# Spreading the last w_out steps of a fused attention and FFN kernel, and holding its second products to a later tick

## The chip, the core and the metric

One core of a Trainium2 chip runs the whole kernel. The metric is the device time of one execution in microseconds (us), as the median of several runs. The engines are named as in the profile: PE (matrix products), DVE and POOL (elementwise work, reductions), ACT (elementwise functions, and a DMA queue of its own), SP (only issues DMAs).

## What is computed

Eight batches of eight attention heads (576 rows, 64 columns each) with a bias that comes from a running sum of `s`, and on the result a gated FFN from 512 to 1536 and back:

```python
def _attn_ref(q, k, v, s):
    scores = scale * np.matmul(q, k.transpose(0, 1, 3, 2))
    cum = np.cumsum(np.maximum(s, 0.0), axis=-1)
    bias = -(cum[:, :, :, None] - cum[:, :, None, :])
    scores = np.where(causal, -1000000000.0, scores + np.minimum(bias, 0.0))
    ...                                   # softmax
    return np.matmul(attn, v).astype(np.float32)

def _moe_ref(x, w_gate, w_val, w_out):
    gate = 1.0 / (1.0 + np.exp(-(x @ w_gate)))
    val = x @ w_val
    return (gate * val @ w_out).astype(np.float32)
```

`x` is the attention's output, 4608 tokens of 512. The three weights of the FFN arrive as float64.

## The kernel before

**Ticks.** 64 heads of five query tiles each make 320 ticks; the loop `for n in range(nticks + 12)` goes through them and emits, for each tick, the scores of one tile (`s_part`, L446 and L447), the bias and the maximum (L461, L471), exponentials (L474), the probabilities p in two halves (L478, L483, L491), their transposition by DMA (pt, L494), the product with v (`av_part`, L506 to L511) and, for a pair of heads, the x of the FFN: `x_part`, `split_x` (L517 to L529), whose last step is a DMA transposition into one of ten x slots. Heads of batch 0 run in another form (names with n_). Slots 0 to 4 exist from the start (NXE is 5); the others are made by `late_slots()` (L189), which closes the pool lp and opens another one in its room. lp holds ws0 (raw words of one weight step) and wa0 (decoded words). x8 and x9, for example, are first used as scratch for the squares of v of batch 2 (load L161 on SP, at ticks from VSQ on).

**FFN.** Tokens are cut into groups of 256; a unit is a group and one of 12 blocks of hidden columns. `ffn_in` multiplies x with w_gate and w_val (tile gv in PSUM, 24 matmuls for a whole group, L657), takes the tanh on ACT (th, L662) and the product on DVE (L664). The units of groups 0 and 1 leave this product in a big tile, t2f. `ffn_mid` scales it by hsc and splits it into two halves h (L672 on ACT, L673 on DVE), `ffn_out` multiplies with w_out (tile o, L687) and, after the 12th block, writes the group's rows by way of an output tile osb (L694, L695).

**Weight steps.** The float64 weights are decoded on the chip in 18 steps: 12 for w_gate and w_val, 6 (12 to 17) for w_out. Each step loads 1 MB of raw words (two DMAs, L253 and L260 on ACT's queue), decodes them (L272 on ACT, L273 to L275 on DVE; the last of them is the last reader of the raw words), sums their squares (L287 on ACT, L289 on POOL), makes a power of two (L125, L127) and writes two rounded halves (L292 on ACT, L293 on DVE; L293 is the last reader of the decoded words). `outroom` says for each of the six w_out steps where its raw words go, where its decoded words go, and behind which step its load may be issued. `hidden_scale()` needs the scales of all 18 steps and gives hsc (L309). No second product can start before it.

**Order.** A planner of the language puts the instructions of each engine in order: it takes the order in which the code emits them as an input, and its own estimate of time as another. Numbers such as ticks therefore do not set the order by hand. Before the change, steps 14 to 17 are emitted with the units of group 1, three steps ahead, which ends by tick 51; in the tick in which the 24th unit is emitted, `hidden_scale`, all 24 held second products and `late_slots` follow. Around that:

```python
outroom = [(4, 0, 0), (5, 0, 0), (0, 0, NF - 3), (3, 0, NF - 1), (5, 0, NF + 1), (0, 0, NF + 2)]
...
                while f >= NF and wnext["step"] < min(f + NF + WLA, len(wsteps)):
                    weight_step()
                emit_unit()
            if state["u"] == 2 * NF:
                hidden_scale()
                while state["o"] < 2 * NF:
                    emit_out()
                late_slots()
```

Of the kernel before, what the change touches and what calls it, by code (L numbers as in the profile page):

```python
# [8 lines left out]
F32 = mybir.dt.float32  # L9
F32R = mybir.dt.float32r  # L10
I32 = mybir.dt.int32
# [5 lines left out]
P = 128  # L17
# [6 lines left out]
def tile_attention_then_gated_ffn(  # L24
# [13 lines left out]
    NT, DM = out.shape  # L38
# [4 lines left out]
    NF = DFF // P  # L43
# [13 lines left out]
    cp = ctx.enter_context(tc.tile_pool(name="cp", bufs=1))  # L57
# [109 lines left out]
    def v_square_sum(b, c):  # L167
        t = vsq.pop((b, c))
        pin(nc.scalar.activation(t, t, AF.Square, accum_out=vss[b][:, c : c + 1]))
# [13 lines left out]
    fp = ctx.enter_context(tc.tile_pool(name="fp", bufs=2))  # L183
    lstack = ctx.enter_context(ExitStack())
    lp = lstack.enter_context(tc.tile_pool(name="lp", bufs=1))
    NX, NXE = 10, 5
    xslots = [cp.tile([P, 2, NTL * P], F16, name=f"x{i}") for i in range(NXE)] + [None] * (NX - NXE)

    def late_slots():  # L189
        lstack.close()  # L190
        xp = lstack.enter_context(tc.tile_pool(name="xp", bufs=1))
        for i in range(NXE, NX):
            xslots[i] = xp.tile([P, 2, NTL * P], F16, name=f"x{i}")
# [17 lines left out]
            c += n  # L211

    raw0 = lp.tile([P, 8 * P, 2], I32, name="ws0")
    dec0 = lp.tile([P, 8 * P], I32, name="wa0")
    flat = w2all.rearrange("p f l h x n -> p (f l h x n)").bitcast(I32)
    raw = [raw0] + [flat[:, i * 16 * P : (i + 1) * 16 * P].rearrange("p (n t) -> p n t", t=2) for i in range(2)]
    dec = [dec0] + [flat[:, i * 8 * P : (i + 1) * 8 * P] for i in range(4, 6)]
# [1 line left out]
    wsteps = [(0, f) for f in range(NF)] + [(1, f) for f in range(0, NF, 2)]  # L219
# [2 lines left out]

    for i in (1, 2):
        raw.append(t2big[:, 8 * i * GT : 8 * (i + 1) * GT].bitcast(I32).rearrange("p (n t) -> p n t", t=2))
    outroom = [(4, 0, 0), (5, 0, 0), (0, 0, NF - 3), (3, 0, NF - 1), (5, 0, NF + 1), (0, 0, NF + 2)]

    def room(n):

        o, f = wsteps[n]
        if o == 0:  # L230
            return raw[f % 3], dec[f % 3], n - 3
        i, j, last = outroom[f // 2]
        return raw[i], dec[j], last
# [61 lines left out]
    def inverse_weights(o, fs):  # L295
        inverse_pow2(invw[:, o, fs], wscale[:, o, fs])

    def hidden_scale():


        inverse_weights(1, slice(0, NF))
        g = wp.tile([P, NF], F32, tag="hsg", name="hsg")
        nc.vector.tensor_tensor(g, invw[:, 0], invw[:, 1], ALU.mult)
        m = wp.tile([P, 1], F32, tag="hsm", name="hsm")
        nc.vector.tensor_reduce(m, g, mybir.AxisListType.X, ALU.max)
        nc.vector.tensor_scalar(gmax, m, 2.0 ** -100, None, ALU.max)
        r = wp.tile([P, 1], F32, tag="hsr", name="hsr")
        nc.vector.reciprocal(r, gmax)
        nc.vector.tensor_scalar(hsc, g, r, 2.0 ** -16, ALU.mult, ALU.mult)  # L309
        out_scale(0)  # L310
# [3 lines left out]
    def out_scale(b):  # L314
        osc[b] = wp.tile([P, 1], F32, tag="osc", name=f"osc{b}", bufs=3)
        nc.vector.tensor_scalar(osc[b], gmax, sv[b][1], 2.0 ** 15, ALU.mult, ALU.mult)

    wnext = {"load": 0, "step": 0}

    def weight_step():  # L320
        n = wnext["step"]
        while n and wnext["load"] < len(wsteps) and room(wnext["load"])[2] < n:
            if not NF <= wnext["load"] < NF + 2:
                load_weight(wnext["load"])
            wnext["load"] += 1
        split_weight(n, decode_weight(n))
        wnext["step"] = n + 1
# [310 lines left out]
    def pieces_of(g):  # L638
        a, e = g * GT, min((g + 1) * GT, NT)
        r = []  # L640
        while a < e:
            b = a // S
            z = min(e, (b + 1) * S)
            r.append((a - g * GT, z - g * GT, b))
            a = z
        return r, e - g * GT
# [29 lines left out]
    def ffn_out(g, f):  # L676
        pcs, n = pieces_of(g)
        if g < 2:
            ffn_mid(g, f)
        h = hst.pop((g, f))  # L680
        for tt in range((n + P - 1) // P):
            m = min(P, n - tt * P)
            if f == 0:
                ops_[g, tt] = pp.tile([P, 512], F32, tag="o", name=f"o{g}_{tt}")
            ps = ops_[g, tt]
            for c, (hl, wl) in enumerate(((0, 0), (0, 1), (1, 0))):
                nc.tensor.matmul(ps[:m], h[:, hl, tt * P : tt * P + m], w2[f][:, wl],  # L687
                                 start=(f == 0 and c == 0), stop=(f == NF - 1 and c == 2))
            if f == NF - 1:
                o = fp.tile([P, DM], F32, tag="io", name=f"osb{g}_{tt}", bufs=2)  # L690
                for a, e, b in pcs:
                    a, e = max(a - tt * P, 0), min(e - tt * P, P)
                    if a < e:
                        nc.scalar.activation(o[a:e], ps[a:e], AF.Copy, scale=osc[b][a:e])  # L694
                nc.gpsimd.dma_start(out[g * GT + tt * P : g * GT + tt * P + m, :], o[:m])  # L695
                del ops_[g, tt]
# [3 lines left out]
    state = {"u": 0, "o": 0}  # L700
# [8 lines left out]
    def emit_out():  # L709
        if state["o"] < len(units):  # L710
            ffn_out(*units[state["o"]])
            state["o"] += 1
# [10 lines left out]
    NE, NOFF = 44, 87  # L723
    FPT = 1.5
    EARLY = 18
    VSQ = 65
    OUT = (22, 30)
    WLA = 3
    nticks = NTL * NH
    for n in range(nticks + 12):  # L730
# [13 lines left out]
        if 2 <= n < nticks + 2:  # L744
            a, z = divmod(n - 2, NTL)
# [5 lines left out]
        if 1 <= n < nticks + 1:  # L751
            a, z = divmod(n - 1, NTL)
# [7 lines left out]
        if 3 <= n < 3 + NTL * NN:  # L760
            with first():
                a, z = divmod(n - 3, NTL)
# [11 lines left out]
        if i < NH:  # L774
            p, j = divmod(i, 2)
# [80 lines left out]
            elif b == 1:  # L856
                if VSQ <= n < VSQ + vch:
                    v_square(2, n - VSQ)
                if VSQ + 5 <= n < VSQ + 5 + vch:
                    c = VSQ + 4 + vch - n  # L860
                    v_square_sum(2, c)
                if n == VSQ + 11:
                    v_scale(2)
# [12 lines left out]
        if n >= NE and state["u"] < 2 * NF:  # L876
            fdone = min(NF, int((n - NE + 1) * FPT))
            while state["u"] < 2 * fdone:
                f = state["u"]
                if f < NF and f % WLA == 0:  # L880
                    while wnext["step"] < f + WLA:
                        weight_step()
                    inverse_weights(0, slice(f, f + WLA))
                    ffn_scale(0, slice(f, f + WLA))
                while f == 8 and wnext["step"] < NF + 1:
                    weight_step()
                while f >= NF and wnext["step"] < min(f + NF + WLA, len(wsteps)):
                    weight_step()
                emit_unit()
            if state["u"] == 2 * NF:  # L890
                hidden_scale()
                while state["o"] < 2 * NF:
                    emit_out()
                late_slots()
        if (n - 30) % (NTL * H) == 0 and n >= 30 + NTL * H:
            ffn_scale((n - 30) // (NTL * H))
        m = n - (11 if n > 2 * NTL * H + 30 else 7)
# [40 lines left out]
```

## Time and profile before

| | us |
|---|---|
| median of 3 runs | 1154.59 |
| lowest and highest | 1151.61, 1155.06 |
| the profiled execution | 1150.75 |
| its span, first to last instruction | 1149.0 |
| PE busy | 1093.9 (95%) |
| DVE, ACT, POOL busy | 774.6, 748.6, 261.9 |

The span is 1.75 us shorter than the profiled execution's own time. All starts below are counted from the span's start. Idle time of an engine is the length of a stretch less its busy time in it; a wait names the instruction that stood still and what came last of what it waited for. A DMA's row on SP is the time that SP took to issue it, not the transfer.

### The profile page before, as it was taken

How to read it: one execution, taken by the hardware profiler on the slowest of the kernel's cores; microseconds unless marked ns; L12 is line 12 of the kernel's file. 1: busy time of each engine (PE TensorE's matmuls, PEld its weight loads, DVE VectorE, ACT ScalarE, POOL GpSimd, SP SyncE). 2: the span in 40 equal slices, each digit the busy share in tenths (PEclk: the TensorE clock that was granted, in tenths of full speed). 3: DMA queues.
4: the chain of work that ended last, by engine and by line, in shares of the span. 5: the costliest groups of instructions: out<-in, count | busy, mean ns of one | idle time of the engine just before them, and what ended most of it. 6: DMA issues, size and time to landing. Idle time of an engine off the chain costs nothing.

```text
span 1149.0 us, 30327 instructions
## 1 busy us (share of the span) xinstructions
PE 1093.9 (95%) x11644; PEld 856.3 (75%) x11644; DVE 774.6 (67%) x2393; ACT 748.6 (65%) x1465; POOL 261.9 (23%) x570
## 2 busy tenths in 40 slices
PE   6787889989999999999999999999999999999997
PEld 4566677758777887788777777778877887787775
DVE  6889899866777777775565677777777775222221
ACT  6989778667677777676665677767776765233222
POOL 5625233222132222121211122212222221000000
PEclk9879899999999999999999999999999999999999
DMA  9776778996989888778646488868887764000000
GB/s 266 214 212 164 178 144 183 185 186 135 165 170 174 165 173 169 141 146 145 137 81 136 89 183 164 162 145 181 145 162 144 142 123 88 13 20 19 1 19 19
DMA packets 445102, 157.62 MB, mean 137 GB/s; under 512 B 403551, under 2 KB 435295, under 8 KB 444958
## 3 DMA queue, kind: packets, MB, share of 16 engines
q1 hardware_dynamic: 418398, 127.12, 57.1%
q10 hardware_dynamic: 23040, 16.78, 4.9%
q0 software_dynamic: 3520, 11.80, 3.0%
q8 instruction: 91, 1.49, 0.6%
q14 instruction: 53, 0.43, 0.1%
HBM read 56.92 MB, written 9.58 MB: 58 GB/s over the span
## 4 chain that ended last, share of the span: by engine, by line
PE 51%; issue 25%; DMA 6%; DVE 5%; ACT 3%; POOL 2%; SPq 1%; POOLq 0%; ACTq 0%; DVEq 0%
PE gv L657 28%; PE o L687 14%; PE s L447 2%; PE s L446 2%; DMA v<-in_v_dram 2%; DMA qk<-in_q_dram 1%; POOL rl L461 1%; PE av L506 1%; PE av L508 1%; DVE e L471 1%; PE av L507 1%; DMA pt<-p 1%; SPq L420 1%; ACT e L474 1%; PE av L510 1%
## 5 line engine op out<-in xcount | busy, mean ns | idle before, releaser
L657 PE MATMUL gv<-x,w 128*128 128x256 f16 (+3 forms) x6912 | 613.5, 246 | 5.4 <-DVE t2f L664 2.9
L657 PEld LDWEIGHTS <-w 128*128 128x128 f16 x6912 | 534.0, 98 | 61.7 <-issue 5.3
L687 PE MATMUL o<-w2all,h 128*128 128x512 f16 x1296 | 314.8, 379 | 0.0
L461 POOL TENSOR_SCALAR_AFFINE_SELECT rl<-rl 128x64 f32<-128x64 f32 (+1 forms) x280 | 111.3, 398 | 519.6 <-DVE em L471 464.3
L474 ACT ACTIVATE e<-e,em 128x576 f32<-128x576 f32 x280 | 154.7, 554 | 92.5 <-DVE em L471 90.5
L687 PEld LDWEIGHTS <-h 128*128 128x128 f16 x1296 | 123.7, 98 | 108.0 <-issue 1.7
L662 ACT ACTIVATE th<-gv,scb 128x256 f32<-128x256 f32 (+3 forms) x288 | 111.2, 411 | 138.4 <-PE gv L657 137.6
L664 DVE SCALAR_TENSOR_TENSOR t<-th,gv 128x256 f32<-128x256 f32 x192 | 80.0, 417 | 132.8 <-ACT th L662 131.6
L471 DVE CUSTOM_DVE_ANT_0 e<-s,rl,qkcf 128x288 f32<-128x288 f32 x280 | 135.6, 485 | 29.9 <-PE s L447 24.5
L672 ACT ACTIVATE h<-t,hsc 128x256 f16<-128x256 f32 x192 | 96.6, 503 | 80.1 <-DVE t L664 80.0
L483 DVE SCALAR_TENSOR_TENSOR p<-e,p 128x384 f16<-128x384 f32 x224 | 101.9, 494 | 40.1 <-ACT p L478 39.3
L673 DVE SCALAR_TENSOR_TENSOR h<-t,hsc,h 128x256 f16<-128x256 f32 x192 | 93.1, 485 | 43.4 <-ACT h L672 43.0
L478 ACT ACTIVATE p<-e 128x1152 f16<-128x1152 f32 x112 | 112.1, 1001 | 3.2 <-DMA pt<-p 0.5
L506 PE MATMUL av<-v,pt 128*128 128x65 f16 x560 | 68.0, 193 | 5.3 <-DMA pt<-p 5.3
L446 PE MATMUL s<-T 128*128 128x288 f16 (+2 forms) x246 | 64.8, 281 | 5.2 <-DMA T<-qk 3.8
L695 POOL DMA_DIRECT2D out_dram<-osb x36 | 20.4, 566 | 212.1 <-ACT osb L694 211.2
L507 PE MATMUL av<-v,pt 128*128 128x64 f16 x560 | 68.0, 192 | 0.0
L508 PE MATMUL av<-v,pt 128*128 128x65 f16 x560 | 68.0, 194 | 0.0
L447 PE MATMUL s<-T 128*128 128x288 f16 (+2 forms) x246 | 61.8, 279 | 1.7 <-DMA T<-T 1.6
L506 PEld LDWEIGHTS <-pt 128*128 128x128 f16 x560 | 52.4, 97 | 11.8 <-DMA pt<-p 6.9
L409 POOL PARTITION_BROADCAST cr<-cr x63 | 58.1, 923 | 4.1 <-DMA cr<-cum_d 4.0
L455 DVE TENSOR_SCALAR rl<-cr,qkcf 128x576 f32<-128x576 f32 x56 | 29.1, 519 | 40.0 <-POOL cr L409 39.8
(155 smaller groups left out, 1440.7 us busy)
## 6 DMA issues: line engine op xcount, KB each, us to landing
out_dram<-osb POOLq DMA_DIRECT2D x36, 256.0 KB, 2.9
v<-v SPq DMA_DIRECT2D x56, 162.5 KB
v<-in_v_dram SPq DMA_DIRECT2D x64, 128.0 KB
T<-T SPq DMA_DIRECT2D x82, 72.0 KB
t2f<-in_v_dram SPq DMA_DIRECT2D x20, 288.0 KB
qk<-in_q_dram SPq DMA_DIRECT2D x17, 288.0 KB
qk<-in_k_dram SPq DMA_DIRECT2D x17, 288.0 KB
w2all<-in_moe_w_gate_dram ACTq DMA_DIRECT2D x7, 512.0 KB
```

What stands on the lines that cost most here:

```text
L446: nc.tensor.matmul(ps[:, : b_ - a], lhs, T[i][:, 0, a:b_], start=True, stop=False)
L461: nc.gpsimd.affine_select(rl[i][:, q0:w], rl[i][:, q0:w], pattern=[[-1, m]], compare_op=ALU.is_ge, fill=-MASKED if i < NN else MASKED, bas ...
L471: nc.vector.tensor_tensor_reduce(e_t[t][:, a:b_], ps[:, : b_ - a], rl[i][:, a:b_], c, init, ALU.add, ALU.min, acc)
L474: nc.scalar.activation(e_t[t][:, :w], e_t[t][:, :w], AF.Exp, bias=init, scale=-1.0)
L478: nc.scalar.activation(p_s[h_][:, 0], e_s[h_], AF.Copy, scale=PSCALE)
L483: nc.vector.scalar_tensor_tensor(flat[:, LOW[t] * P : (LOW[t] + t) * P], e_t[t][:, : t * P], PSCALE, flat[:, kb * P : (kb + t) * P], ALU.m ...
L506: nc.tensor.matmul(AV[i][:, t], hi, v_[:, D : 2 * D + 1], start=kb == 0, stop=False)
L657: nc.tensor.matmul(ps[:, gv, a:e], w1[f][:, cc, gv, wl], x_of(b, cc)[:, xl, c0 + a : c0 + e], start=(c == 0), stop=(c == 3 * NC - 1))
L662: nc.scalar.activation(th[:, a:e], ps[:, 0, a:e], AF.Tanh, scale=scb[b][:, f : f + 1])
L672: nc.scalar.activation(h[:, 0], t2, AF.Copy, scale=hsc[:, f : f + 1])
L673: nc.vector.scalar_tensor_tensor(h[:, 1], t2, hsc[:, f : f + 1], h[:, 0], ALU.mult, ALU.subtract)
L687: nc.tensor.matmul(ps[:m], h[:, hl, tt * P : tt * P + m], w2[f][:, wl], start=(f == 0 and c == 0), stop=(f == NF - 1 and c == 2))
```

## The change

1. x slots that exist from the start: six in place of five; four are left for `late_slots`.
2. A tile osb in the permanent pool takes the place of the output tiles and, as dec0, of wa0: the decoded words lie in the output's room. In lp only ws0 is left.
3. The last two of `outroom`: step 16 loads into ws0 behind step 14, step 17 into the same ws0 behind step 16. Before, they used part of t2f and ws0.
4. Steps 14 to 17 are emitted at ticks 50, 54, 58 and 62; `hidden_scale`, the held second products and `late_slots` at tick 66 (NOUT). The squares of v of batch 2 start at tick 68 and not 65.

```diff
-    NX, NXE = 10, 5
+    NX, NXE = 10, 6
@@
     raw0 = lp.tile([P, 8 * P, 2], I32, name="ws0")
-    dec0 = lp.tile([P, 8 * P], I32, name="wa0")
+    osb = cp.tile([P, 2, DM], F32, name="osb")
+    dec0 = osb.rearrange("p a n -> p (a n)").bitcast(I32)
@@
-    outroom = [(4, 0, 0), (5, 0, 0), (0, 0, NF - 3), (3, 0, NF - 1), (5, 0, NF + 1), (0, 0, NF + 2)]
+    outroom = [(4, 0, 0), (5, 0, 0), (0, 0, NF - 3), (3, 0, NF - 1), (0, 0, NF + 2), (0, 0, NF + 4)]
@@
-                o = fp.tile([P, DM], F32, tag="io", name=f"osb{g}_{tt}", bufs=2)
+                o = osb[:, tt % 2]
@@
-    VSQ = 65
+    NW, NOUT = 50, 66
+    VSQ = 68
@@
-                while f >= NF and wnext["step"] < min(f + NF + WLA, len(wsteps)):
+                while f >= NF and wnext["step"] < NF + 2:
                     weight_step()
                 emit_unit()
-            if state["u"] == 2 * NF:
-                hidden_scale()
-                while state["o"] < 2 * NF:
-                    emit_out()
-                late_slots()
+        while NF + 2 <= wnext["step"] < min(NF + 3 + (n - NW) // 4, len(wsteps)):
+            weight_step()
+        if n == NOUT:
+            hidden_scale()
+            while state["o"] < 2 * NF:
+                emit_out()
+            late_slots()
```

The lines of the changed kernel are one higher from L215 on (L310 is L309 of before). In the rows below, the digits behind a name are the planner's numbers of the tiles. On DVE, around the end of `hidden_scale` (gmax and hsr lead to hsc), there stood before, from row 412 on:

```order
L471 ISA em12_2_0_2934 128x1
L305 TENSOR_REDUCE hsm_2380<-hsg_2378 128x1
L306 TENSOR_SCALAR gmax_113<-hsm_2380 128x1
L293 SCALAR_TENSOR_TENSOR w2all_78<-wa0_137,wscale_111,w2all_78 128x1024
L308 RECIPROCAL hsr_2383<-gmax_113 128x1
L316 TENSOR_SCALAR osc0_2386<-gmax_113,vin0_328 128x1
L471 ISA e_0_79,em12_1_0_2949<-s12_1_0_2922,rl12_2814,qkcf6_2679 128x192
L471 ISA em12_1_0_2949 128x1
L316 TENSOR_SCALAR osc1_3132<-gmax_113,vin1_1006 128x1
L365 TENSOR_SCALAR qk0_7_2952<-qkt7_2941 128x2
L309 TENSOR_SCALAR hsc_112<-hsg_2378,hsr_2383 128x12
```

and now, from row 416 on:

```order
L665 SCALAR_TENSOR_TENSOR t2f_136<-th1_1_1934,gv1_1_1909 128x256
L131 TENSOR_SCALAR invw_110<-wscale_111 128x12
L472 ISA e_0_79,em12_0_0_2724<-s12_0_0_2692,rl12_2548,qkcf6_2385 128x64
L472 ISA em12_0_0_2724 128x1
L304 TENSOR_TENSOR hsg_2804<-invw_110 128x12
L306 TENSOR_REDUCE hsm_2806<-hsg_2804 128x1
L307 TENSOR_SCALAR gmax_113<-hsm_2806 128x1
L309 RECIPROCAL hsr_2809<-gmax_113 128x1
L317 TENSOR_SCALAR osc0_2812<-gmax_113,vin0_329 128x1
L317 TENSOR_SCALAR osc1_3126<-gmax_113,vin1_1007 128x1
L310 TENSOR_SCALAR hsc_112<-hsg_2804,hsr_2809 128x12
```

hsc moves from row 422 to row 426; the last L293 (step 17, reading the decoded words) moves from row 415 to row 434, behind hsc.

On ACT, step 17's raw words (the DMA into ws0) were issued before right behind the square of step 14 (wss14), from row 212 on:

```order
L287 ACTIVATE w2all_78,wss14_1886<-wa0_137 128x1024
L253 DMA ws0_136<-in_moe_w_out_dram 128x8x128
L474 ACTIVATE e_1_80<-e_1_80,em9_4_1_1557 128x576
L260 DMA ws0_136<-in_moe_w_out_dram 128x8x128
L662 ACTIVATE th0_0_1374<-gv0_0_1349,scb0_1347 128x256
```

Now the load that stands there is step 16's, and that of step 17 stands behind the square of step 16 (wss16), from row 252 on. Its reader, the first L273 of step 17, is row 267:

```order
L288 ACTIVATE w2all_78,wss16_2530<-osb_138 128x1024
L254 DMA ws0_137<-in_moe_w_out_dram 128x8x128
L261 DMA ws0_137<-in_moe_w_out_dram 128x8x128
L388 ACTIVATE qk16_12_2420<-qk32_6_2220,qksc6_2383 96x6x64
L390 ACTIVATE qk16_12_2420<-qk32_6_2220,qksc6_2383 96x6x64
L663 ACTIVATE th0_9_1794<-gv0_9_1769,scb0_1348 128x256
L475 ACTIVATE e_0_79<-e_0_79,em11_2_0_2523 128x320
L663 ACTIVATE th0_10_1822<-gv0_10_1797,scb0_1348 128x256
L293 ACTIVATE w2all_78<-osb_138,wscale_111 128x1024
L475 ACTIVATE e_0_79<-e_0_79,em11_1_0_2545 128x192
L475 ACTIVATE e_0_79<-e_0_79,em11_0_0_2559 128x64
```

The load moved from row 213 to row 253, 14 rows ahead of its reader; before, the reader was row 259.

On PE, the first second product o0_0 stood behind unit gv1_3, from row 1412 on:

```order
L657 LDWEIGHTS w1_3_69
L657 MATMUL gv1_3_2029<-x3_133,w1_3_69 128x256
L657 LDWEIGHTS w1_3_69
L657 MATMUL gv1_3_2029<-x3_133,w1_3_69 128x256
L687 LDWEIGHTS h0_0_2388
L687 MATMUL o0_0_2391<-w2all_78,h0_0_2388 128x512
L687 LDWEIGHTS h0_0_2388
L687 MATMUL o0_0_2391<-w2all_78,h0_0_2388 128x512
```

and now, from row 1460 on:

```order
L447 LDWEIGHTS T13_2575
L447 MATMUL s13_2_0_3050<-T13_2575 128x320
L448 LDWEIGHTS T13_2575
L448 MATMUL s13_2_0_3050<-T13_2575 128x320
L658 LDWEIGHTS w1_4_70
L658 MATMUL gv1_4_2002<-x3_133,w1_4_70 128x256
L658 LDWEIGHTS w1_4_70
L658 MATMUL gv1_4_2002<-x3_133,w1_4_70 128x256
L688 LDWEIGHTS h0_0_2814
L688 MATMUL o0_0_2817<-w2all_78,h0_0_2814 128x512
```

The first second product moved from row 1417 to row 1469, behind one more unit, gv1_4, and behind scores of head 13.

## Rows read from the trace of the kernel before

**Rows 1.** The page, section 1: engine, busy us, share of the span, instructions.

```profile
PE 1093.9 (95%) x11644; PEld 856.3 (75%) x11644; DVE 774.6 (67%) x2393; ACT 748.6 (65%) x1465; POOL 261.9 (23%) x570
```

**Rows 2.** Busy time by stage: stretch, its length, each engine, PEclk, DMA share, GB/s.

```profile
119.00:190.00 71.00, 59.89 (x621) 49.86 (x620) 64.77 (x197) 55.48 (x100) 22.64 (x43) 0.95 0.79 170
190.00:241.00 51.00, 47.72 (x477) 35.05 (x475) 42.73 (x148) 39.59 (x78) 15.93 (x31) 1.00 0.96 187
241.00:303.00 62.00, 57.65 (x724) 42.99 (x723) 42.51 (x135) 41.89 (x88) 14.31 (x30) 1.00 0.77 162
...
430.00:985.00 555.00, 555.00 (x6282) 436.88 (x6281) 388.98 (x1260) 371.22 (x723) 113.93 (x274) 1.00 0.72 139
...
145.00:165.00 20.00, 17.03 (x181) 14.56 (x179) 17.63 (x51) 15.39 (x28) 6.45 (x11) 1.00 0.68 136
165.00:190.00 25.00, 21.81 (x254) 18.58 (x252) 23.37 (x78) 19.79 (x37) 7.80 (x16) 1.00 0.77 165
```

**Rows 3.** Waits of PE, 119 to 190 us: us in total, times, longest us.

```profile
PE gv L657 <- DVE t2f L664: 2.9, 3, 1.7
...
PE nx_ps L629 <- DVE nx L615: 0.6, 1, 0.6
```

**Rows 4.** Waits of PE, 190 to 303 us.

```profile
PE s L447 <- DMA t2f<-t2f: 2.1, 1, 2.1
PE av L506 <- DMA pt<-p: 1.6, 1, 1.6
PE gv L657 <- DMA x<-x: 1.6, 1, 1.6
```

**Rows 5.** Instructions by tile (ws, w2all, hsc): ns min/median/max, first and last start.

```profile
L272 ACT ACTIVATE wa<-ws x6: 1111/1138/1157, 11.2 to 169.6; 128x1024 f32<-128x1024 f32 x6
L275 DVE SCALAR_TENSOR_TENSOR wa<-ws,wa x6: 1216/1219/1251, 14.7 to 176.9; 128x1024 int32<-128x1024 int32 x6
...
L260 ACTq DMA_DIRECT2D ws<-in_moe_w_out_dram x2: 682/768/854, 81.0 to 132.2; - x2
...
L293 DVE SCALAR_TENSOR_TENSOR w2all<-wa,wscale,w2all x6: 1258/1274/1285, 110.3 to 183.5; 128x1024 f16<-128x1024 f32 x6
...
L309 DVE TENSOR_SCALAR hsc<-hsg,hsr x1: 229/229/229, 185.4 to 185.4; 128x12 f32<-128x12 f32 x1
...
L687 PE MATMUL o<-w2all,h x1296: 377/379/380, 190.4 to 1142.0; 128*128 128x512 f16 x186
```

**Rows 6.** PE, from 231 us: start us, us, instruction, count.

```profile
231.21 1.58 PE L657 MATMUL gv<-x,w 128*128 128x256 f16 x13
```

**Rows 7.** ACT by line and shape, 160 to 190 us: count, busy us, mean ns.

```profile
L662 ACT ACTIVATE th<-gv,scb 128x256 f32<-128x256 f32 x8 | 3.7, 458 | 0.6 <-PE gv L657 0.6
...
L292 ACT ACTIVATE w2all<-wa,wscale 128x1024 f16<-128x1024 f32 x2 | 2.3, 1136 | 0.0
...
L387 ACT ACTIVATE qk<-qk,qksc 96x384 f16<-96x384 f32 x3 | 1.8, 614 | 1.4 <-DMA T<-qk 0.7 <-DVE qksc L371 0.7
...
L478 ACT ACTIVATE p<-e 128x768 f16<-128x768 f32 x2 | 1.7, 840 | 0.0
...
L474 ACT ACTIVATE e<-e,em 128x192 f32<-128x192 f32 x3 | 1.3, 445 | 0.0
```

**Rows 8.** SP's DMA issues: start us, us that the issue took, queue, line, transfer.

```profile
182.65 0.24 SPq L406 DMA_DIRECT2D cr<-cum_d  x1
184.78 0.84 SPq L161 DMA_DIRECT2D x<-in_v_dram  x2
...
232.69 0.65 SPq L347 DMA_DIRECT2D qk<-in_k_dram  x1
...
241.03 1.28 SPq L494 DMA_TRANSPOSE pt<-p  x1
242.40 2.16 SPq L529 DMA_TRANSPOSE x<-x  x1
```

**Rows 9.** Waits of DVE, 119 to 190 us.

```profile
DVE xe_w L125 <- POOL wtot L289: 2.5, 3, 1.2
```

## Prediction

> **What bounds the kernel now.** The page comes first. PE is busy for 1093.9 of the 1149.0 us of the span [rows 1], so at most 55 us of idle PE could be won. The busy time by stage shows where they lie [rows 2]: in each stretch, idle PE is its length less PE's busy time. From 119 to 190 us that is 11.1 us, from 190 to 241 us 3.3, from 241 to 303 us 4.35, and from 430 to 985 us nothing at all: there PE works without a gap. The change can move the time only by what it does to the gaps before about 430 us.
>
> Where the change can act is read from the orders of both kernels. On every engine the instructions are the same ones; up to the first unit (gv0_0, about 119 us, the start of the second stretch) they stand in the same places, and from the scores of head 19 on they do again. Total work of PE, DVE and ACT is thus constant. The question is what happens to the 11.1 + 3.3 + 4.35 = 18.7 us of gaps in between.
>
> Next come the waits of PE. Before 190 us the longest belonging to the FFN is that of the gate matmuls for DVE's product (2.9 us) [rows 3]; DVE is busy for 23.37 of the 25 us from 165 to 190 [rows 2], so it limits this stage almost as much as PE. After 190 us no wait is for h or for hidden_scale: PE waits for transposed probabilities (1.6), a transposed x (1.6) and a swapped half of T (2.1) [rows 4]. The second products started at 190.4 us, 5 us after hidden_scale's result hsc (185.4 us) [rows 5]. They are filler that was ready, not something PE stood still for.
>
> **The change, part by part.**
>
> *The spread and the hold (ticks 50, 54, 58, 62 and 66).* The text of the kernel moves step 17 by 11 ticks and the second products by 15. The order does not: hsc moves from row 422 of DVE to 426, and DVE's work ahead of it is equal within 0.2 us, summed over the rows with the durations of the trace. On PE the first second product falls 52 rows further on, behind one more unit, gv1_4, and the scores s13_2. That is 24 matmuls at about 0.12 us (13 of them in a row take 1.58 us [rows 6]), an estimate of 2.9 us, and two for scores: about 3 us of PE work. This work is moved and not added. It costs nothing if gv1_4 can run at once: it needs the gv bank that DVE's product of gv1_2 frees. By DVE's new order that product ends at about 190 us, the moment when PE is through with gv1_3. Cover and need meet; a miss costs up to about 2 us (the longest wait of this kind was 1.7 us, in the group of 2.9), a gain is not to be had from it. I take 0, since DVE's work up to there is equal.
>
> *Step 17 reloads ws0.* Before, the last step's raw words were issued at 132 us at the latest, 37 us ahead of their reader at 169.6 us [rows 5]. Now step 16 uses the same room, and the load waits for step 16's last reader (L275), issued from ACT behind the square of step 16. How long is the transfer? 1 MB, and the core moved 165 GB/s from 165 to 190 us [rows 2]: 6.4 us; at the rate of 136 GB/s of the stretch before it would be 7.7 us. What covers it? In ACT's new order there stand between the issue and the reader four scalings (4 x 0.61), three tanh (3 x 0.46), one w_out rounding (1.14), one p (0.84) and three e (0.34 to 0.55, mean 0.445): 2.44 + 1.37 + 1.14 + 0.84 + 1.34 = 7.1 us [rows 7]. So the load is covered by 0.7 us of ACT work, or missed by 0.6 us. DVE, too, has other work in the meantime. I take 0 for it; the ends are 0 and +0.6, and more if the transfer is slowed (the slower rival).
>
> The Trainium skill, DMA: Bandwidth & Descriptors, Rules for kernel authors, says to issue a DMA early, compute, and wait late, so that its cost is overlapped. It speaks against this part, which issues a load some 30 us later than before. By it alone the 6.4 us would lie open; by the rows, ACT's work lies beside it.
>
> *Step 16's load and the earlier two.* They go where they went or into ws0 in place of a part of w2all; same size, same engine: 0.
>
> *Decoded words in osb, the sixth early x slot.* Only addresses change. The output tiles are first written when a group's second products are complete, long after the decode. x5 can be transposed without waiting for the late slots; but group 2 needs x4 to x7, and x7 is the last: 0.
>
> *The late slots and SP's queue.* Before, SP stood still from 182.89 us (182.65 + 0.24) to 184.78 us with the loads for the v squares behind it [rows 8]: they wait for the room of wa0, which step 17's L293 reads last (183.5 + 1.27 = 184.8 us) [rows 5]. After, only ws0 must be free, whose last reader L275 ended at 178.1 us (176.9 + 1.22). SP gets up to 1.9 us ahead. Much of that SP gives back: it waits in turn for p, and a transposition is not issued before. What stays is that one load of in_k (0.65 us [rows 8]) now stands behind the transposition of x7 and not ahead of it. x7's was issued at 242.40 us, straight behind pt's (241.03 + 1.28) [rows 8], and PE waited 1.6 us for it. This wait should shrink by 0.65; its ends are 0 and -1.6.
>
> The next wait is the 2.1 us for a swapped t2f, T of head 20 [rows 4]. It decides what is kept: PE's end moves by as much as this chain does. The scores that feed it come 0.65 us earlier, and the in_k load that moved is by then issued in both orders, so I let the chain ride along: -0.65. Its ends are 0 (the chain is SP's own and stays) and -2.1.
>
> The Trainium skill, DMA: Bandwidth & Descriptors, Issuing engines are not separate DMA queues, holds that the time a sequencer takes to issue is usually small relative to the transfer. Here it is not: one transposition held SP for 1.28 to 2.16 us [rows 8], so the order on SP counts. If the rule held here, the term above would be 0.
>
> *Early, at 122 to 131 us.* The second matmul of s9_4 now stands ahead of the transposition nx_ps, which waited 0.6 us for DVE [rows 3]; it may wait some 1 us longer. On the other side DVE waits 2.5 us, in three pieces, for the sums of POOL's reduce [rows 9], and with the steps further apart part of that goes. I take 0 with ends -1.5 and +1.5; a delay here is partly swallowed by the waits behind it.
>
> **Sum:** 0 + 0 + 0 - 0.65 + 0 = -0.65 us. The profiled run took 1150.75 us; that gives 1150.1. The median of the runs shown, 1154.59, is 3.84 us above the profiled run; on that scale the forecast is 1153.9 us. A measurement of this kernel can tell about 0.3% (3.5 us) from no change, so the forecast is "the same". The sum of the ends is -1.5 - 2.1 - 0 = -3.6 and +2 + 0.6 + 1.5 = +4.1: 1151.0 to 1158.7.
>
> **Rivals.**
>
> *Faster: the attention chain gets its lead.* Scores of head 13 now stand ahead of the second products. If that lets softmax, p and their transpositions run ahead, the gaps from 190 to 303 us, 3.28 + 4.35 = 7.6 us [rows 2], go. For it: all waits there are for products of that chain [rows 4]. Against: DMA queues and SP are what these waits end on, and SP issues as much as before. All of it gives 1154.6 - 7.6 = 1147.0 us; it is "faster" from half of it on.
>
> *Slower: the reload of ws0 comes late.* Place: ACT's L272 of step 17. ACT works in order, so behind it wait tanh of gv1_0, e of head 12 and thus the gv banks and the scores of PE. If the transfer, with other queues busy (DMA share 0.77 [rows 2]), takes twice 6.4 us, 12.8 - 7.1 = 5.7 us are open. DVE has little slack there, so nearly all reaches PE: 1153.9 + 5.7 = 1159.6 us. It is "slower" from a transfer of 11 us on; up to 7.1 us nothing is seen.
>
> *The change does what its text says.* Were steps and products really held to ticks 50 to 66, DVE would be eased from 165 to 190 us, where PE idles 3.2 us, and from 145 to 165 us, where it idles 3.0 [rows 2]: up to 6.2 us less, 1148.4 us. The order speaks against it (four rows on DVE), and I count it with the faster rival.
>
> **Chances.** Forecast, no visible change: 0.66. Faster rivals: 0.22. Slower rival: 0.12. The range leaves out about a half of each rival, at their far ends: 1147.5 to 1158.5. The likeliest case alone has 1151.0 to 1158.1, where the bound of a visible loss lies.
>
> **What would show it.** The steps and hsc at the same times as before (hsc within 2 us of 185.4, the first second product between 191 and 194 us) shows the first part right. L272 of step 17 with no DMA wait ahead of it shows the reload covered; a DMA wait on ws of several us on ACT is the slower rival. The loads for the v squares issued before 184 us and a shorter wait for x7 show SP's term. If idle PE from 190 to 303 us falls from 7.6 to under 4 us, the faster rival holds. Idle PE of 119 to 190 us well over 11 us, or a wait of second products for h, would make the forecast wrong from a side I have not priced.

## The result and the profile after

The change makes the kernel slower: 1159.32 us (median of 20 runs) against 1154.62 us of the kernel before, a ratio of 1.0042 (95% interval 1.0028 to 1.0057), 4.7 us. The forecast was 1153.9 us and no visible change; the time lies beyond the upper end of the range, 1158.5 us.

PE's total, which answers to [rows 1], and DVE's hardly differ in the page of the changed kernel:

```profile
PE 1097.7 (95%) x11644; PEld 858.0 (74%) x11644; DVE 776.5 (67%) x2393; ACT 748.9 (65%) x1465; POOL 261.9 (23%) x570
```

The profiled execution of the changed kernel has a span of 1158.8 us, 9.8 more than that of before. Not all of this is the change. Up to the scores of head 8, where both kernels have the same order, it is 4.6 us late already (120.23 us against 115.67 us for the first of them). Executions of one kernel differ by several us, and a part of it arises there. So each trace below is cut at three points of PE's own work that every order has: the first score of head 8 (s8), the first matmul of unit gv1_1, and the last 288 columns of the scores of head 19 (s19), behind which all orders agree again. The rows are busy times by stage, s8 to gv1_1 and gv1_1 to s19: stretch, its length, busy us of each engine (count), granted clock (PEclk), DMA share, GB/s. The kernel before:

```profile
115.67:181.00 65.33, 54.22 (x543) 45.02 (x543) 58.93 (x165) 48.80 (x84) 20.54 (x36) 0.92 0.79 166
181.00:273.73 92.73, 87.88 (x901) 64.18 (x899) 72.43 (x245) 69.97 (x140) 26.34 (x54) 1.00 0.86 178
```

The kernel before in a second trace (run f1 below):

```profile
114.33:179.93 65.60, 54.81 (x543) 45.44 (x544) 59.17 (x167) 48.75 (x84) 20.29 (x37) 0.93 0.78 165
179.93:274.73 94.80, 88.08 (x900) 63.96 (x898) 72.56 (x242) 70.11 (x140) 25.63 (x54) 1.00 0.87 174
```

The changed kernel:

```profile
120.23:183.92 63.69, 53.90 (x540) 44.96 (x541) 54.90 (x157) 47.30 (x82) 16.79 (x33) 0.95 0.80 158
183.92:283.09 99.17, 90.59 (x909) 64.64 (x906) 77.49 (x253) 70.94 (x140) 28.04 (x57) 0.98 0.86 172
```

And the changed kernel in a second trace (run e4):

```profile
114.59:179.44 64.85, 54.02 (x540) 45.17 (x541) 54.89 (x157) 47.38 (x82) 17.04 (x33) 0.94 0.80 155
179.44:276.95 97.51, 88.83 (x909) 64.38 (x906) 78.35 (x253) 70.70 (x140) 27.59 (x57) 1.00 0.91 175
```

What to see: the second stretch takes 92.7 and 94.8 us before, 99.2 and 97.5 us after. DVE's work there was 72.4 and 72.6 us and is 77.5 and 78.4 us: some 5 us more, and these come out of the first stretch, where DVE falls from about 59 to 54.9 us. The sum of both stretches is nearly the same (131.4 and 131.7 us before, 132.4 and 133.2 us after). So some 4 to 6 us of DVE's work have moved behind the start of gv1_1.

Which work that is, DVE's own rows tell (start us, us, instruction). The kernel before, step 17 (its L273 to L275, then L293) between the products L664 of the gate units; the last but one row is the product of gv1_0:

```profile
172.37 0.69 DVE L273 TENSOR_SCALAR w2all<-wa 128x1024 int32<-128x1024 int32 x1
...
174.63 1.22 DVE L274 SCALAR_TENSOR_TENSOR wa<-wa,w2all 128x1024 int32<-128x1024 int32 x1
...
176.87 1.22 DVE L275 SCALAR_TENSOR_TENSOR wa<-ws,wa 128x1024 int32<-128x1024 int32 x1
...
181.77 0.42 DVE L664 SCALAR_TENSOR_TENSOR t2f<-th,gv 128x256 f32<-128x256 f32 x1 [0.45 <-ACT th L662]
...
183.47 1.28 DVE L293 SCALAR_TENSOR_TENSOR w2all<-wa,wscale,w2all 128x1024 f16<-128x1024 f32 x1
```

The changed kernel (lines one higher); the three products L665 are those of gv1_0, gv1_1 and gv1_2:

```profile
183.20 0.69 DVE L274 TENSOR_SCALAR w2all<-osb 128x1024 int32<-128x1024 int32 x1
...
184.24 1.22 DVE L275 SCALAR_TENSOR_TENSOR osb<-osb,w2all 128x1024 int32<-128x1024 int32 x1
185.38 0.41 DVE L665 SCALAR_TENSOR_TENSOR t2f<-th,gv 128x256 f32<-128x256 f32 x1
...
186.21 1.22 DVE L276 SCALAR_TENSOR_TENSOR osb<-ws,osb 128x1024 int32<-128x1024 int32 x1
...
190.72 0.41 DVE L665 SCALAR_TENSOR_TENSOR t2f<-th,gv 128x256 f32<-128x256 f32 x1
...
192.23 0.22 DVE L310 TENSOR_SCALAR hsc<-hsg,hsr 128x12 f32<-128x12 f32 x1
...
193.92 1.27 DVE L294 SCALAR_TENSOR_TENSOR w2all<-osb,wscale,w2all 128x1024 f16<-128x1024 f32 x1
...
196.45 0.41 DVE L665 SCALAR_TENSOR_TENSOR t2f<-th,gv 128x256 f32<-128x256 f32 x1
```

Before, the three decode instructions (3.1 us) were through with DVE at 178.1 us, ahead of the start of gv1_1 (181.0 us), and the last rounding ahead of the product of gv1_1. Now two of the three (2.4 us) run behind the start of gv1_1 (183.9 us), the last rounding (193.92 us) behind its product, and the product of gv1_2 (196.45 us) behind all of them. Unit gv1_4 needs the bank that this product frees. Rows of PE (idle time before it and what ended it in brackets):

```profile
193.43 1.26 PE L658 MATMUL gv<-x,w 128*128 128x256 f16 x10
196.91 2.56 PE L658 MATMUL gv<-x,w 128*128 128x256 f16 x22 [2.22 <-DVE t2f L665]
```

This wait of 2.22 us did not exist before: second products, which go to other banks, stood there. It comes in all three traces of this order (2.2, 1.9 and 2.3 us). The waits of PE from gv1_1 to s19 (line, what it waited for, us in total, times, longest). The kernel before:

```profile
PE av L506 <- DMA pt<-p: 1.6, 1, 1.6
PE gv L657 <- DMA x<-x: 1.6, 1, 1.6
PE s L446 <- DMA T<-qk: 0.9, 1, 0.9
PE s L447 <- DMA T<-T: 0.7, 1, 0.7
```

The changed kernel:

```profile
PE av L507 <- DMA pt<-p: 3.7, 3, 2.5
PE gv L658 <- DVE t2f L665: 2.2, 1, 2.2
PE s L448 <- DMA T<-T: 2.0, 3, 0.8
PE s L447 <- DMA T<-qk: 0.6, 1, 0.6
```

The wait for x7 (1.6 us before) is gone in this trace, but pt, T and the gate units cost more. The wait for the swapped half of T in [rows 4] (2.1 us) lies behind s19 in both kernels. Of the transfer into ws0 there is nothing to see. ACT's waits from 160 to 200 us hold no DMA but one for T:

```profile
ACT e L475 <- DVE em L472: 4.1, 3, 2.9
ACT qk L388 <- DMA T<-qk: 3.2, 1, 3.2
ACT th L663 <- PE gv L658: 1.1, 1, 1.1
ACT w2all L288 <- DVE osb L276: 0.4, 1, 0.4
```

The reader L273 of step 17 started at 181.8 us, 11.7 us behind the issue of the load's second half (170.1 us):

```profile
L273 ACT ACTIVATE osb<-ws x7: 1128/1134/1154, 10.1 to 181.8; 128x1024 f32<-128x1024 f32 x7
```

```profile
L261 ACTq DMA_DIRECT2D ws<-in_moe_w_out_dram x3: 677/686/737, 85.0 to 170.1; - x3
```

What stands ahead of this reader on ACT is a scaling of qk that waited for a transposed T (start us, us, instruction, idle time before it):

```profile
179.71 0.61 ACT L388 ACTIVATE qk<-qk,qksc 96x384 f16<-96x384 f32 x1 [3.17 <-DMA T<-qk]
...
181.82 1.13 ACT L273 ACTIVATE osb<-ws 128x1024 f32<-128x1024 f32 x1
```

The load of step 16 moved as well. Before, it was the last of three into t2f; now it goes into ws0 (the first row is by tile, with first and last start; the second is of the changed kernel):

```profile
L253 ACTq DMA_DIRECT2D t2f<-in_moe_w_out_dram x3: 547/547/584, 85.5 to 118.2; - x3
```

```profile
138.01 0.55 ACTq L254 DMA_DIRECT2D ws<-in_moe_w_out_dram  x1
```

Counted from s8, that is 2.6 us before and 17.8 us now. Step 16's last rounding on DVE starts at 52.5 us behind s8 before and at 55.8 us now.

### The profile page after: what moved, and what is told of

The parts are those of the page before. It is cut to its first block, busy times and chain, and to the rows that moved or that the text cites. A ratio compares the mean times of both kernels' runs of the same rounds, so it can differ in the third digit from the quotient of the medians.

```text
span 1158.8 us, 30337 instructions
## 1 busy us (share of the span) xinstructions
PE 1097.7 (95%) x11644; PEld 858.0 (74%) x11644; DVE 776.5 (67%) x2393; ACT 748.9 (65%) x1465; POOL 261.9 (23%) x570
## 4 chain that ended last, share of the span: by engine, by line
PE 59%; issue 21%; DMA 6%; ACT 5%; DVE 5%; POOL 2%; SPq 1%; ACTq 0%; POOLq 0%; DVEq 0%
PE gv L658 31%; PE o L688 17%; PE s L448 3%; PE s L447 3%; PE na_ps L606 1%; DMA T<-qk 1%; PE av L509 1%; PE av L507 1%; PE av L508 1%; DMA pt<-p 1%; DVE e L472 1%; DMA T<-T 1%; DMA v<-in_v_dram 1%; ACT e L588 1%; DVE p L484 1%
## 5 line engine op out<-in xcount | busy, mean ns | idle before, releaser
L665 DVE SCALAR_TENSOR_TENSOR t<-th,gv 128x256 f32<-128x256 f32 x192 | 80.2, 417 | 132.2 <-ACT th L663 131.2
L448 PE MATMUL s<-T 128*128 128x288 f16 (+2 forms) x246 | 61.6, 279 | 3.4 <-DMA T<-T 3.4
```

The costliest lines, as they stand in the source:

```text
L448: nc.tensor.matmul(ps[:, : b_ - a], lhs, T[i][:, 2, a:b_], start=False, stop=True)
```

## The experiments

Ratios are to the kernel before on the same chip, medians in us; the interval of a ratio is at 95%.

### Which part of the change it is

**Both rooms alone** (run e1: no sixth slot, no spread, no hold):

```diff
-    dec0 = lp.tile([P, 8 * P], I32, name="wa0")
+    osb = cp.tile([P, 2, DM], F32, name="osb")
+    dec0 = osb.rearrange("p a n -> p (a n)").bitcast(I32)
-    outroom = [..., (5, 0, NF + 1), (0, 0, NF + 2)]
+    outroom = [..., (0, 0, NF + 2), (0, 0, NF + 4)]
-                o = fp.tile([P, DM], F32, tag="io", name=f"osb{g}_{tt}", bufs=2)
+                o = osb[:, tt % 2]
```

> The kernel before with two edits of the change alone: decoded words in osb (and no wa0), and the last two rooms of outroom, so that steps 16 and 17 load into ws0. No sixth early x slot, no spread, no hold, squares of v at tick 65 as before. Every engine's order is the changed kernel's, but for three rows on SP. Theory 1 (the rooms cost it, the ticks do nothing): slower than before by 3 to 6 us, as the whole change (4.7 us). Theory 2 (spread, hold or the sixth slot cost it): within 1 us of before.

Measured: 1158.85 against 1154.15, ratio 1.0035 (1.0016 to 1.0053). Within the intervals that is the whole loss. Neither ticks nor hold are needed for it; without them the traces show the same order on PE, DVE and ACT as with them. Theory 1 holds.

**The reload alone** (run e2: the last two rooms of outroom, decoded words in wa0 as before):

> The kernel before with the last two rooms of outroom alone: steps 16 and 17 load into ws0, decoded words stay in wa0. Step 17's words arrive late and its place on ACT and DVE is the changed kernel's, but the first second product stays at row 1417 of PE, ahead of unit gv1_4. Theory A (the late load of step 17 costs the time, by moving its decode behind 180 us, where DVE is full): slower by 3 to 6 us. Theory B (it takes the second products behind gv1_4, which then waits for DVE's product): within 1.5 us of before, since that order is not here. Theory C (the room of the decoded words alone): within 1 us.

Measured: 1156.65, ratio 1.0025 (1.0007 to 1.0044): slower, if by somewhat less than the 3 to 6 us of theory A. Its second stretch:

```profile
182.62:279.51 96.89, 90.00 (x908) 65.13 (x905) 77.41 (x253) 70.28 (x140) 28.32 (x57) 0.98 0.89 173
```

Here the second products stand ahead of gv1_4 as before; DVE still has 77.4 us in the second stretch, and PE waits in other places (3.5 us for T, 1.7 us for h). So a loss is there without the wait of gv1_4, which is one form of it: that speaks against theory B, though the lower end of the interval (0.8 us) lies within the 1.5 us that B allows.

**The room of the decoded words alone**, twice (runs e3 and h3):

> The kernel before with the decoded words in osb alone; outroom, ticks and slots of before. Hidden scale stays at row 422 of DVE, the first second product at row 1417 of PE; the loads for the squares of v move two places up on SP, and the scores of head 13 ahead of gv1_4. Theory A: within 1 us of before. Theory C (the room of the decoded words, which reorders SP's loads and the transpositions behind them): slower by 3 us or more. Theory B: within 1.5 us.

> The kernel before with the decoded words in osb alone, once more (first time 0.16% slower, -0.07 to 0.38%). Its step 17 stands ahead of the product of gv1_1, as before. If the place of step 17 is all: within 1 us of before. If the room has a share of its own: 1.5 to 3 us slower again.

Measured: first 1156.30 against 1154.15, ratio 1.0016 (0.9993 to 1.0038), unclear; then 1154.52 against 1154.28, ratio 0.9998 (0.9976 to 1.0020). No share of its own is seen, but up to 0.2% by the second measurement isn't excluded. The second stretch of its first trace is like that of before, with DVE at 72.6 us:

```profile
181.91:275.57 93.66, 88.02 (x900) 64.07 (x898) 72.61 (x243) 69.55 (x140) 25.02 (x54) 1.00 0.87 176
```

**The change again** (run e4):

> The changed kernel once more, beside the others on the same chip: slower than before by 3.3 to 6.6 us (0.28 to 0.57%), as measured. Its trace shows which of the gaps of the first one come back: the wait of gv1_4 for DVE's product (2.2 us) and the one for pt near 242 us (2.5 us, with a lower granted clock behind it) if they belong to the order; not the 4.5 us by which the first trace was late at the first unit, where the order is the one of before.

Measured: 1158.57, ratio 1.0030 (1.0010 to 1.0051). The wait of gv1_4 came back (1.9 us), that for pt too, but with 1.6 us in place of 2.5.

**The kernel before again** (run f1):

> The kernel before, once more: a ratio of 1 (0.9985 to 1.0015), and a second trace of it. Counted from the first score of head 8 (same order up to there), its hsc should again come at 69.7 us, its first second product at 74.7 us and its end at 1033 us, within 1.5 us; the traces of the changed order end 3.3 to 9.0 us later by this count. If this one is 3 us or more off, the single traces can't carry the comparison.

Measured: 1154.88 against 1156.03, ratio 0.9990 (0.9972 to 1.0009). Counted from s8, its end comes at 1033.8 us, that of the first trace at 1033.3; both of the changed kernel come at 1038.5 and 1036.6. But the first trace of osb alone ends at 1036.6 us by this count and that of f2 below at 1038.9, and by their runs neither kernel is shown to be slower. Single traces show where time goes; how much a kernel costs is taken from its runs.

### Why the reload costs

**Step 17's decode taken out**, of the changed kernel (run f2), of before (f3), and of the kernel with the reload alone (h2):

```diff
         nc.scalar.activation(a.bitcast(F32), r[:, :, 1].bitcast(F32), AF.Copy, scale=2.0 ** -112)
+        if n == len(wsteps) - 1:
+            return a.bitcast(F32)
```

> The changed kernel without DVE's three decode instructions of step 17 (L274 to L276, 3.1 us); the last sixth of w_out is then not what it should be. Theory A (the late decode of step 17 overloads DVE where the gate units begin): most of the 4.5 us comes back, within 1.5 us of the kernel before, and no wait of gv1_4 for DVE's product. Rival (the reload's transfer, or SP's and DMA's order around 170 to 245 us, costs it): still slower than before by 3 us or more, with the waits for pt, T and x as they are.

> The kernel before without the same three instructions of step 17, as the control of the run above. Theory A: DVE is full from 165 to 190 us here too, so up to 1.5 us faster than before, and the changed kernel without them within 1.5 us of this one. Rival: this one gains as much as the changed kernel does, and the two stay 3 us or more apart.

> The kernel before with the two rooms of outroom alone, and without DVE's three decode instructions of step 17; the last sixth of w_out is not what it should be. On DVE the last rounding of step 17 stands at row 413, ahead of the product of gv1_1 (427). Place or amount: within 1.5 us of before, where the reload alone was 2.5 us slower. If the reload costs by its DMAs: 2 to 4 us slower still.

Measured: the change without it 1154.95 against 1156.03, ratio 1.0008 (0.9987 to 1.0029); before without it 1155.16, ratio 0.9998 (0.9977 to 1.0020); the reload without it 1154.83 against 1154.28, ratio 1.0003 (0.9985 to 1.0021). In the kernel before, 3.1 us of DVE work are worth nothing; in the changed order they are worth the loss, within these intervals (that of h2 overlaps with that of the reload alone, so the pair of the change and f2 carries more of it). In all three the last rounding of step 17 stands ahead of the product of gv1_1, and no unit waits 0.5 us or more for DVE's product in the second stretch. A rival is the late end of `hidden_scale`, which holds back the second products. It doesn't fit: hsc starts 72.6 and 71.6 us behind s8 in f2 and h2, about as late as in the change (72.0 and 73.2 us) and the reload alone (71.1 us), and f2 and h2 are not shown to be slower. Against a full match: the trace of f2 is a long execution (span 1158.3 us) and shows new waits for T and pt; the time of that experiment rests on its 12 runs.

**Its load taken out**, decode left in (run f4):

```diff
-            if not NF <= wnext["load"] < NF + 2:
+            if not NF <= wnext["load"] < NF + 2 and wnext["load"] < len(wsteps) - 1:
```

> The changed kernel without the two loads of step 17; it decodes step 16's words once more, so the last sixth of w_out is not what it should be. ACT's reader of step 17 stays at the same row (265 for 267). Theory A (the place of the decode): still slower than before by 2 us or more. Rival (the transfer of 1 MB at 170 us itself, in the way of the transpositions): within 1.5 us of before.

Measured: 1160.49 against 1156.03, ratio 1.0054 (1.0033 to 1.0074). Slower with no transfer at all: the 1 MB at 170 us and its queue are not what costs. Step 17's decode is as late as with it: its first instruction on ACT starts 61.9 us behind s8 (61.6 us in the change, 53.9 us before). So its own load isn't what makes it late either. A unit again waits 1.7 us for DVE's product:

```profile
PE av L507 <- DMA pt<-p: 1.9, 3, 1.2
PE gv L658 <- DVE t2f L665: 1.7, 1, 1.7
```

**The decode of step 17 made longer**, in the kernel before (run g1) and in the changed one (g2):

```diff
         nc.vector.tensor_scalar(m, a, 3, 0x7FFFFFF8, ALU.logical_shift_left, ALU.bitwise_and)
+        for _ in range(4 if n == len(wsteps) - 1 else 0):
+            nc.vector.tensor_scalar(m, a, 3, 0x7FFFFFF8, ALU.logical_shift_left, ALU.bitwise_and)
```

> The kernel before with one instruction of step 17's decode on DVE (L273, 0.69 us, which gives the same result again) done five times in place of once: 2.8 us more of DVE work and a decode that ends later, with rooms, loads and ticks of before. The first second product moves far behind gv1_4. Theory A (step 17's work on DVE in the stretch where the gate units of group 1 begin is what counts): slower than before by 2 to 5 us, with PE's gate units waiting for DVE's products between 60 and 90 us behind the first score of head 8. Rival (only the reload and the order of DMAs that it brings cost time; DVE has room): within 1 us of before.

> The changed kernel with the same four repetitions of L274 in step 17, 2.8 us more of DVE work. Theory A: slower than before by 6 to 9 us, as much above the change as the run above is above the kernel before, or more. Rival: as the change, 3.5 to 6 us.

Measured: before with it 1161.38 against 1156.03, ratio 1.0054 (1.0034 to 1.0075): with a longer decode that ends late the old rooms are as slow as the new ones, and the units wait three times for DVE's product. More than the decode moves here: hsc comes 89.1 us behind s8 (69.7 before) and the first second product at 106.8 us (74.7 before). Waits of PE in its second stretch:

```profile
PE gv L659 <- DVE t2f L666: 3.3, 3, 1.3
PE s L449 <- DMA T<-T: 2.0, 1, 2.0
PE av L508 <- DMA pt<-p: 1.9, 2, 1.5
```

But the change with it has 1157.36, ratio 1.0026 (1.0001 to 1.0051), not the 6 to 9 us that theory A expected; the planner found another order for it, with hsc at 87.7 us and the first second product at 90.5 us behind s8 (72.0 and 79.6 us in the change). More work on DVE does not add to the loss in proportion.

**Step 16's decode taken out** of the changed kernel (run h1), the same 3.1 us:

> The changed kernel without DVE's three decode instructions of step 16 (3.1 us) in place of step 17's; a sixth of w_out is then not what it should be. Step 17's last rounding stays behind the product of gv1_1 on DVE (row 436 for 426). If the place of step 17's decode is what counts: slower than before by 2 to 5 us. If the amount of DVE work is: within 1.5 us of before, as without step 17's.

Measured: 1158.12 against 1154.28, ratio 1.0039 (1.0017 to 1.0061). The time is what "place, not amount" expected. Its trace doesn't show it at the place, though: the second stretch is 95.0 us with 74.3 us of DVE, and the largest wait is one of 4.7 us for pt in the first stretch:

```profile
118.13:186.95 68.82, 58.09 (x546) 47.72 (x547) 56.67 (x161) 48.92 (x86) 18.86 (x36) 0.85 0.84 160
186.95:281.98 95.03, 88.60 (x900) 63.85 (x897) 74.28 (x246) 69.28 (x138) 25.21 (x54) 1.00 0.90 173
```

```profile
PE av L509 <- DMA pt<-p: 4.7, 1, 4.7
PE s L449 <- DMA T<-qk: 1.8, 1, 1.8
```

So this run excludes that less DVE work in general is enough, and leaves open by which wait it is slow. Step 16's last rounding is back at 52.1 us behind s8 here (52.5 before), yet step 17's first instruction on ACT still starts at 60.4 us: a late rounding of step 16 is not needed for a late step 17.

### The second products at high priority

In the changed kernel (run g3) and in the one before (g4):

```diff
-            hidden_scale()
-            while state["o"] < 2 * NF:
-                emit_out()
+            with first():
+                hidden_scale()
+                while state["o"] < 2 * NF:
+                    emit_out()
```

> The changed kernel with hidden_scale and the held second products emitted at high priority. On PE the first second product moves only from row 1469 to 1465, but the second products of the first tile pair end sooner and group 2 begins 150 rows later. Theory A: still slower than before by 3 to 6 us, since step 17 stays where it is. Rival (the second products that stand too late among the gate units cost it): within 2 us of before.

> The kernel before with the same high priority for hidden_scale and the second products: group 2, and with it the wait for x7 (1.6 to 2.3 us in the traces so far), begins 160 rows of PE later, by when x7 should be there. If that wait is worth its length: 1 to 2 us faster than before. Rival: the waits for pt, T and t2f take its place, within 1 us of before.

Measured: the change with it 1156.76 against 1156.03, ratio 1.0016 (0.9995 to 1.0037), which decides neither way; before with it 1156.39, ratio 1.0008 (0.9986 to 1.0030). In the trace of the latter the wait for x7 is gone and waits for DVE's maximum (em, 3.3 us) and its xq (1.5) are there instead: the rival. No version here beats the kernel before.

## Why the forecast was wrong, point by point

**That the ticks do nothing** was right, and stronger than I said: spread, hold, sixth slot and the squares' tick leave the order as it is (e1). What I had put down as a change of ticks was an effect of the rooms.

**The start of the second products, taken at 0 with a miss of about 2 us, is the first step that failed.** I compared DVE's work ahead of hsc, found it equal within 0.2 us, and concluded that the bank of gv1_4 comes free in time. hsc was the wrong mark. The mark was the product of gv1_1 on DVE: before, it stood behind step 17's last rounding (row 423 for 415), now it stands ahead of it (row 416 for 434), so that this rounding lies between the products of gv1_1 and gv1_2. Equal work up to hsc says nothing of what stands between the gate units' products, which free PE's banks. The need came as forecast: PE was through with gv1_3 74.5 us behind s8 (190 less 115.67 is 74.3). The cover did not: the product of gv1_2 ended at 76.6 us, and not at 74.3. Before, it ended at 75.6 us; there second products, standing ahead of gv1_4, hid the difference. The miss measured 1.9 to 2.3 us in the three traces and is about half of the loss. The rest is later waits for pt and T (second stretch 3 to 6 us longer in all), which I had left at the old size. The signs that I had named say the same: hsc came 72.0 and 73.2 us behind s8 in the two traces of the change (69.7 before; I had allowed 2 us), the first second product at 79.6 and 80.7 us (74.7 before), on the scale of before at 195.2 and 196.4 us and not from 191 to 194 us.

**The reload, taken at 0 with an end of +0.6, is the second.** The transfer was covered, as I had it: no wait for ws0, and no gain without it (f4). The work of ACT that I had counted as cover, 7.1 us, took 11.7 us, since ACT also waited there, 3.2 us of it for T. What the term left out is the place of step 17's decode: on ACT and DVE it came 8 to 9 us later, counted from s8 (ACT's first instruction at 53.9 us before, at 61.6 and 62.7 us in the two traces of the change), into the first units of group 1. The run with the reload alone shows that this costs time by itself: there the second products stand ahead of gv1_4, the first miss does not arise, and the kernel is 2.5 us slower (0.8 to 5.1 by the interval). I also took step 16's load at 0, as one of the same size on the same engine, and named its old room wrongly (it was a part of t2f, not of w2all); it is issued 15 us later behind s8 than before. The Trainium skill, DMA: Bandwidth & Descriptors, Rules for kernel authors, advises to issue a DMA early, to compute, and to wait for it late, which overlaps its fixed setup cost. That a load issued late would lie open was my reading of it; here the transfer did not, 11.7 us passed between issue and reader. My slower rival named the right part (ws0 taken twice), and that its time (1159.6 us) is nearly the measured one is luck: its price, an open transfer, is not what was paid. It got a chance of 0.12 because I asked only whether the transfer fits.

**SP's lead, -0.65 us,** was not kept. The loads for the squares were issued 1 us earlier, counted from s8 (188.35 less 120.23 us, before 184.78 less 115.67), and the wait for x7 did shrink (none, and 0.7 us in the second trace). But the next wait, for t2f, stayed at 2.2 and 2.1 us, so the end of 0 held, and the lead was of no use.

**The early term, 0 with ends of 1.5 us,** held for the two traces of the change: up to gv1_1 they take 63.7 and 64.9 us, before 65.3 and 65.6. In e1, of the same order, it took 67.6 us. There PE waited 2.1 us for T of head 10, whose transposition is now followed at once on SP by one for pt. Such a wait, of 1.8 to 2.1 us, stands in six of the ten traces with the new order at this place, and in none of the seven with the old one (0.74 us at most). Two of these six are the kernels without step 17's decode, which are not slower; so it is not what decides, but it is a risk that the sum lacked.

**The faster rival** needed idle PE of 7.6 us from 190 to 303 us to fall. From gv1_1 to s19 idle PE (length less busy) was 4.9 and 6.7 us before and is 8.6 and 8.7 us.

**What stays open:** which of the two rooms makes step 17 late (no run has one of them alone), why more DVE work in step 17 does not add to the changed kernel (g2), and by which wait h1 is slow. The planner makes another order for each edit, so an experiment that changes the work changes places, too.

## What to carry to other kernels

When a buffer is taken twice, ask not only whether the second transfer fits, but also where the work that waits for it lands on the other engines, and what stands behind it there. Compare two orders by the instructions that free the bound engine's buffers (here DVE's product of each unit), not by the one that the change names. Where a planner sets the order, look first at whether an edit of emission order reaches it at all; here no edit of ticks did, and the one that gives two steps another room made the loss.

## What was not expected of the hardware

Behind some waits of PE the granted clock fell. In the changed kernel's first trace PE waited 2.48 us for pt until 242.77 us, and the granted clock of the stretches of 5 us from 240 to 250 us was 0.82 and 0.83, so part of PE's work there ran at 1.2 and not 2.4 GHz; in its second trace the same wait was 1.6 us, until 237.4 us, and the clock behind it stayed at 1.00 (the first fence is of the first trace, the other of the second):

```profile
240.00:245.00 5.00, 2.52 (x30) 1.35 (x27) 3.50 (x13) 1.94 (x4) 0.90 (x5) 0.82 1.17 213
245.00:250.00 5.00, 5.00 (x24) 2.14 (x23) 2.09 (x10) 4.65 (x11) 0.41 (x1) 0.83 0.87 172
```

```profile
240.00:245.00 5.00, 5.00 (x29) 2.50 (x28) 3.35 (x13) 4.92 (x12) 0.41 (x1) 1.00 1.16 155
```

The same happened in run e1: the wait of 2.1 us for T of head 10 was followed by a granted clock of 0.65 from 151 to 154 us. The length of a wait doesn't settle it: the 2.22 us for DVE's product until 196.91 us in the changed kernel's first trace were followed by a granted clock of 1.00 (195 to 205 us), and so were 2.15 us in the first trace of before (until 298.2 us; 1.00 from 295 to 305 us) and 2.49 us in run g4 (until 302.4 us; 1.00 from 300 to 310 us). Where the clock falls, the cost is more than the wait: PE is busy for 90.6 us in the second stretch of the changed kernel's first trace and for 88.8 us in that of its second, with the same 909 matmuls. No term of the sum had that.
